# Mixer and MLP block: the first two tiles centred before the first product and scaled behind it, w1 loaded in quarters, two tiles transposed by DMA

## Chip, cores and metric

The kernel runs on one core of a Trainium2 chip. The metric is the device time of one launch in microseconds (us); smaller is better. Before the change three runs took 138.89, 138.96 and 139.11, median 138.96.

## What is computed

For x of 2048 rows by 512 columns, bfloat16, with weights w1, w2 (512 x 512), w3 (512 x 1792) and w4 (1792 x 512):

```python
h = gelu(layernorm(x) @ w1)              # layernorm over a row, no scale or offset
# the four column quarters g0..g3 of h are shifted by -1, +1, -2, +2 rows, zeros at the ends
hs = concatenate([g0, g1, g2, g3], axis=-1) @ w2
x1 = x + hs
out = x1 + gelu(layernorm(x1) @ w3) @ w4
```

layernorm is (x - mean) / sqrt(var + 1e-5), gelu its tanh approximation.

## The kernel before, in words

**Tiles.** Row r of x is row r // 16 of tile r % 16, so there are 16 tiles of 128 rows, and a shift of the rows by one is a step to the neighbouring tile. A product needs its input with the 512 columns on the partitions, so each normalized tile (xn) is transposed into xT, in one of two ways: four TensorE transposes into a PSUM bank and a copy out by ScalarE (ACT), steps tp (line 456) and evA (468); or a DMA transpose that SyncE (SP) issues, dT (444).

**Layernorm of a tile.** VectorE (DVE) takes statistics (st, 328) and makes mean and variance of them (ag, 331). GpSimd (POOL) adds epsilon and takes the power -1/2 (rs, 354 and 363, for one tile or two). DVE subtracts the mean and multiplies by that (norm, 434). For tile 2 the sums are taken by ACT instead (sum, dev, with vp, vpd and pw on POOL).

**First product** (m1, 507). A pair of tiles is taken at once: w1's blocks are the stationary operand, xT of the pair (256 columns) the moving one, so h comes out transposed, in two PSUM banks, and one gelu on ACT (g1, 568) writes it to hT. Pair 0 (m1x, 524) is computed tile by tile and input block by input block, 128 columns at a time, into four banks; its gelu is three instructions (551, 557), since tiles 0 and 1 lie next to zero columns.

**Second product** (m2, 582). For an output tile t it adds four matmuls, one for each shifted quarter j, which read hT of tiles t-1, t+1, t-2 and t+2. DVE adds x to the result (add, 594), which is x1, and the tiles are normalized again, mostly on ACT (424), and transposed by DMA into x1T.

**Third and fourth product** (609 and 635). Groups of four tiles: w3 against x1T, gelu on ACT (622), then w4, and DVE's last addition (649). From 37 us on nothing else runs on TensorE.

**The order.** Every engine runs its own list in program order and waits by semaphores; what waits for what follows from buffers read and written. The order of the front is written out by hand in HEAD, a list of steps that each append to one engine's list: `tp 0 4` transposes tile 0 into bank 4, `m1x 1 0 2` multiplies tile 1 with input block 2 in the banks from 0, `m1 2 0 3` makes output block 3 of pair 2 in the banks from 0, `m2 5 7 0 1 2 3` is tile 5 in bank 7 with all four quarters. Behind HEAD the order is in calls (lines 762 to 799). All loads are issued by SP, before HEAD: x tiles 0, 1, 2 and 3 one at a time, 4 and 5 together, w1 in two halves, x in 6-7, 8-9, 10-11, 12-15, then w2; w3 follows behind the last transpose of x. w4 comes in four pieces, among the transposes of the last tiles of x1.

**Warm-ups.** keep_warm (667) puts matmuls of ones into a bank nobody reads: 12 at the start, and 2 more (`warm 2 3 1`) between the transposes of tiles 0 and 1.

The start of HEAD, which sets who is behind whom:

```python
st 0; ag 0; rs 0 1; st 1; ag 1; sum 2; st 3; rs 1 1; norm 0; ag 3; tp 0 4; dev 2; vp 3; vpd 2;
st 4; evA 0; norm 1; warm 2 3 1; pw 2 2; tp 1 5; st 5; m1x 0 0 0; m1x 0 0 1; norm 2; evA 1;
```

Of the kernel before, what the change touches and what calls it, by code (L numbers as in the profile page):

```python
# [5 lines left out]
P = 128  # L6
# [4 lines left out]
LN_EPS = 1e-5  # L11
# [149 lines left out]
st 0; ag 0; rs 0 1; st 1; ag 1; sum 2; st 3; rs 1 1; norm 0; ag 3; tp 0 4; dev 2; vp 3; vpd 2;  # L161
st 4; evA 0; norm 1; warm 2 3 1; pw 2 2; tp 1 5; st 5; m1x 0 0 0; m1x 0 0 1; norm 2; evA 1;
m1x 0 0 2; norm 3; ag 4; tp 2 6; ag 5; m1x 0 0 3; rs 4; tp 3 7; evA 2; m1x 1 0 0; st 6;
m1x 1 0 1; m1x 1 0 2; evA 3; m1x 1 0 3; st 7; ag 6; ag 7; m1 1 4 0; rs 6; norm 5; g1 0; norm 4;
m1 1 4 1; tp 5 7; tp 4 6; st 8; evA 5; norm 7; m1 1 4 2; m1 1 4 3; evA 4; st 9; tp 7 7; ag 8;
ag 9; rs 8; norm 6; m1 2 0 0; evA 7; m1 2 0 1; st 11; tp 6 6; g1 1; m1 2 0 3; norm 8; ag 11;
m1 2 0 2; evA 6; m2 2 4 0; st 10; m2 2 4 1; norm 9; ag 10; m1 3 2 1; g1 2; rs 10; m1 3 2 3;
st 13; m1 3 2 0; st 12; ag 13; m1 3 2 2; norm 11; m2 2 4 2; dT 8; m2 2 4 3; st 14; g1 3; norm 10;
m2 3 5 0 1 2 3; dT 9; st 15; ag 12; ag 15; ag 14; rs 12; m2 4 6 0 1 2 3; m1 4 0 1; add 2; dT 11;
m1 4 0 0; rs 14; norm 13; m1 4 0 3; m1 4 0 2; add 3; norm 15; dT 10; norm 14; m2 5 7 0 1 2 3;  # L170
g1 4; norm 12; dT 13; dT 12; dT 15; dT 14
# [3 lines left out]
def bass_standalone__mixer_s_mlp__prompt_kernel(  # L175
# [18 lines left out]
    NO = 4  # L194

# [6 lines left out]
    with ExitStack() as es:  # L202
# [5 lines left out]
        hT = sb("hT", [P, DC, HTW], BF16)  # L208
        h2T = sb("h2T", [P, FC, 2, 512], BF16)
# [5 lines left out]
        sink = sb("sink", [P, D], BF16)  # L215
        tot = sb("tot", [P, NT, 2], F32)
# [117 lines left out]
        g_sd, g_sum, g_nm, g_dev = {}, {}, {}, {}  # L334
        g_vp = [None] * NT
        sink_slot = Slot()
# [35 lines left out]
        def sum_act(q):  # L372

            a, g = src(q)
            g_sum[q], g_nm[q] = Gen(), Gen()
            gs = sink_slot.new()
            pr.op("act", f"sq_sum{q}",
                  lambda e: e.activation(sink[:], a, ACT_F.Identity, accum_out=tot[:, q, 0:1]),
                  r=[g], w=[gs, g_sum[q]])
            pr.op("pool", f"nm{q}",  # L380
                  lambda e: e.tensor_scalar(nmean[:, q : q + 1], tot[:, q, 0:1], -1.0 / D, None,
                                            ALU.mult),
                  r=[g_sum[q]], w=[g_nm[q]])

        def dev_act(q):

            a, g = src(q)
            gs, gd = sink_slot.new(), Gen()
            pr.op("act", f"sq_dev{q}",
                  lambda e: e.activation(sink[:], a, ACT_F.Square, bias=nmean[:, q : q + 1],  # L390
                                         scale=1.0, accum_out=tot[:, q, 1:2]),
                  r=[g, g_nm[q]], w=[gs, gd])
            g_dev[q] = gd

        def vpe_dev(q):

            g_vp[q] = Gen()
            pr.op("pool", f"vpe{q}",
                  lambda e: e.tensor_scalar(vpe[:, q : q + 1], tot[:, q, 1:2], 1.0 / D, LN_EPS,
                                            ALU.mult, ALU.add),  # L400
                  r=[g_dev[q]], w=[g_vp[q]])

        def vpe_bn(q):

            g_vp[q] = Gen()
            pr.op("pool", f"vpe{q}",
                  lambda e: e.tensor_scalar(vpe[:, q : q + 1], mv[:, q : q + 1, 1], LN_EPS, None,
                                            ALU.add),
                  r=[g_mv[q]], w=[g_vp[q]])

        def pow2(q, n):

            pr.op("pool", f"pow{q}",
                  lambda e: e.tensor_tensor(rstd[:, q : q + n], vpe[:, q : q + n],
                                            neghalf[:, 0:n], ALU.pow),
                  r=g_vp[q : q + n] + [g_nh], w=g_rstd[q : q + n])

        def norm(eng, q):
            a, g = src(q)
            s = q % NXN  # L420
            g_xn[q] = xn_slot[s].new()
            if eng == "act":
                pr.op("act", f"norm{q}",
                      lambda e: e.activation(xn[:, s, :], a, ACT_F.Identity,  # L424
                                             bias=nmr[:, q : q + 1], scale=rstd[:, q : q + 1]),
                      r=[g, g_nmr[q], g_rstd[q]], w=[g_xn[q]])
            elif q in g_nm:
                pr.op(eng, f"norm{q}",
                      lambda e: e.tensor_scalar(xn[:, s, :], a, nmean[:, q : q + 1],
                                                rstd[:, q : q + 1], ALU.add, ALU.mult),  # L430
                      r=[g, g_nm[q], g_rstd[q]], w=[g_xn[q]])
            else:
                pr.op(eng, f"norm{q}",
                      lambda e: e.tensor_scalar(xn[:, s, :], a, mv[:, q, 0:1], rstd[:, q : q + 1],  # L434
                                                ALU.subtract, ALU.mult),
                      r=[g, g_mv[q], g_rstd[q]], w=[g_xn[q]])
# [78 lines left out]
        def mm1_tile_by_input(t, b, dc):  # L515

            p = t // 2
            if p not in g_y:
                g_y[p] = ([bank[b + i].new() for i in range(DC)], b)

            def f(e):
                for fc in range(DC):
                    o = 512 * (b + fc) + P * (t % 2)
                    ins = e.matmul(ps[:, o : o + P], w1_sb[:, dc, P * fc : P * (fc + 1)],  # L524
                                   xT[:, dc, P * t : P * (t + 1)],
                                   start=(dc == 0), stop=(dc == DC - 1))
                return ins

            pr.op("pe", f"m1x_{t}_{dc}", f, r=[g_w[("w1", dc)], g_xT[t]], w=g_y[p][0])
# [42 lines left out]
        g_o = {}  # L572

        def mm2(t, b, js=(0, 1, 2, 3)):

            if t not in g_o:
                g_o[t] = (bank[b].new(), b)
            win = [window(j, t) for j in js]

            def f(e):  # L580
                for j, (c, _) in zip(js, win):
                    ins = e.matmul(bankap(b), hT[:, j, c : c + P], w2_sb[:, j, :],  # L582
                                   start=(j == 0), stop=(j == DC - 1))
# [91 lines left out]
        load_x("sp", 2, 1)  # L675
        load_x("sp", 3, 1)
        load_x("sp", 4, 2)
        load_w("w1", w1_sb, w1, 0, 2)
        load_w("w1", w1_sb, w1, 2, 2)
        load_x("sp", 6, 2)  # L680
        load_x("sp", 8, 2)
        load_x("sp", 10, 2)
# [4 lines left out]
        keep_warm(12, 3)  # L687
# [55 lines left out]
        def last_tile():  # L743
# [10 lines left out]
            "warm": lambda n, b, q: keep_warm(n, b, [g_mv[q]]), "sum": sum_act, "dev": dev_act,  # L754
            "vpd": vpe_dev, "vp": vpe_bn, "pw": pow2, "m1x": mm1_tile_by_input,
            "m1": lambda p, b, *fcs: mm1(p, b, fcs), "g1": gelu1,
# [10 lines left out]
        mm2s(4, 4)  # L767
# [13 lines left out]
        for k in (10, 12, 14):  # L781
# [3 lines left out]
            load_w4(2 * (k - 10), 4)  # L785
        wide(0, [2, 3])
        load_w4(12, FC - 12)
# [44 lines left out]
```

## Time and profile before

| | us |
|---|---|
| median of three runs | 138.96 |
| the profiled execution | 138.48 |
| its span, first to last instruction | 136.6 |
| TensorE (PE) busy | 132.6 (97%) |
| VectorE / ScalarE / GpSimd busy | 50.9 / 51.7 / 18.8 |
| TensorE in the chain that ended last | 93% of the span |
| TensorE's first transpose of tile 0 / of tile 1 | 5.88 / 7.87 |
| first matmul of the third product | 37.33 |

The span is shorter than the execution's time by what lies around it (1.88). A line of the timeline gives start and length in us, engine, line of the kernel, operation, out<-in, form and count; in brackets stands how long the engine had been idle before it and who ended that. PEld is TensorE's loading of the stationary operand, which runs beside PE. The length of a PE instruction is from its issue to the end of its result, so lengths overlap; the pitch from one to the next is what counts for a sum. A table by stretch gives for each engine the busy time and the number of instructions, then the granted clock, the share of the DMA engines and GB/s. The DMA view gives for the issues of one kind the KB and the time from issue to landing.

### The profile page before, as it was taken

The numbers are of one execution on the slowest core, as the hardware profiler recorded it, in microseconds if no ns is written. First come the engines' busy times: TensorE is split into PE (matmuls) and PEld (weight loads), VectorE is DVE, ScalarE is ACT, GpSimd is POOL, SyncE is SP. The second block draws the span as 40 slices with busy tenths as digits, with TensorE's granted clock in tenths as the row PEclk, the third lists the DMA queues.
The fourth block names the chain that finished last, engine by engine and source line by source line (L and its number), as shares of the span: only waits on it lengthen the run. The fifth ranks groups of instructions, "written<-read, shape, count | busy, mean of one in ns | idle before, by whom it ended". The sixth has DMA issues, their size and how long they took to land.

```text
span 136.6 us, 1835 instructions
## 1 busy us (share of the span) xinstructions
PE 132.6 (97%) x716; PEld 67.3 (49%) x716; DVE 50.9 (37%) x125; ACT 51.7 (38%) x64; POOL 18.8 (14%) x52
## 2 busy tenths in 40 slices
PE   7979999999999999999999999999999999999993
PEld 3369857664444444444444444444444444444452
DVE  2699889999966610000322000023200002322222
ACT  4558623499535555552000555200055530000000
POOL 2644431553322200000000000000000000000000
PEclk9999999999999999999999999999999999999999
DMA  4996153499845499300111100011110001111121
GB/s 106 275 307 238 38 101 74 96 286 294 174 96 113 89 268 243 135 5 0 38 38 38 38 5 0 0 38 38 38 38 0 5 0 38 38 38 38 39 78 42
DMA packets 20264, 12.18 MB, mean 89 GB/s; under 512 B 13728, under 2 KB 19104, under 8 KB 20256
## 3 DMA queue, kind: packets, MB, share of 16 engines
q1 hardware_dynamic: 20112, 12.03, 33.3%
q8 instruction: 6, 0.10, 0.3%
q10 hardware_dynamic: 144, 0.03, 0.1%
q14 instruction: 2, 0.02, 0.1%
HBM read 6.82 MB, written 2.10 MB: 65 GB/s over the span
## 4 chain that ended last, share of the span: by engine, by line
PE 93%; DMA 3%; SPq 1%; DVE 1%; issue 0%
PE ps L635 35%; PE ps L609 35%; PE ps L582 10%; PE ps L507 9%; DMA x_sb<-in_x_dram 3%; PE ps L524 1%; PE ps L456 1%; SPq L258 1%; DVE st L328 1%; DVE xn L434 0%; DVE o_sb L649 0%
## 5 line engine op out<-in xcount | busy, mean ns | idle before, releaser
L635 PE MATMUL ps<-w_sb,h2T 128*128 128x512 bf16 (+2 forms) x238 | 48.9, 366 | 0.0
L609 PE MATMUL ps<-x1T,w_sb 128*128 128x512 bf16 x224 | 48.8, 379 | 0.0
L622 ACT ACTIVATE h2T<-ps 128x1024 bf16<-128x1024 f32 x28 | 28.7, 1024 | 44.8 <-PE ps L609 44.8
L649 DVE TENSOR_TENSOR o_sb<-ps,x_sb 128x512 bf16<-128x512 f32 (+2 forms) x17 | 11.2, 660 | 75.0 <-PE ps L635 75.0
L635 PEld LDWEIGHTS ps<-w_sb,h2T 128*128 128x128 bf16 x238 | 22.7, 98 | 26.0
L609 PEld LDWEIGHTS ps<-x1T,w_sb 128*128 128x128 bf16 x224 | 22.0, 98 | 26.4
L328 DVE BATCH_NORM_STATS2 st<-x_sb 128x6 f32<-128x512 bf16 x31 | 20.2, 680 | 2.9 <-DMA x_sb<-in_x_dram 2.9
L582 PE MATMUL ps<-w_sb,hT 128*128 128x512 bf16 x64 | 14.8, 379 | 0.0
L507 PE MATMUL ps<-xT,w_sb 128*128 128x256 bf16 x112 | 13.7, 273 | 0.0
L507 PEld LDWEIGHTS ps<-xT,w_sb 128*128 128x128 bf16 x112 | 10.7, 98 | 2.3 <-ACT xT L468 0.2
L363 POOL TENSOR_TENSOR rstd<-vpe,neghalf 128x2 f32<-128x2 f32 (+1 forms) x16 | 11.2, 699 | 0.9
L594 DVE TENSOR_TENSOR x_sb<-ps,x_sb 128x512 bf16<-128x512 f32 x16 | 10.3, 678 | 0.3 <-PE ps L582 0.2
L434 DVE TENSOR_SCALAR xn<-x_sb,mv,rstd 128x512 bf16<-128x512 bf16 x21 | 8.0, 404 | 4.5 <-POOL rstd L363 4.4
L582 PEld LDWEIGHTS ps<-w_sb,hT 128*128 128x128 bf16 x64 | 6.2, 98 | 6.3 <-ACT hT L568 0.3
L424 ACT ACTIVATE xn<-x_sb,nmr,rstd 128x512 bf16<-128x512 bf16 x10 | 7.5, 808 | 3.3 <-POOL nmr L368 3.3
L568 ACT ACTIVATE hT<-ps 128x1024 bf16<-128x1024 f32 x6 | 6.1, 1020 | 5.6 <-PE ps L507 5.6
L354 POOL TENSOR_SCALAR vpe<-mv 128x2 f32<-128x2 f32 (+1 forms) x16 | 3.7, 230 | 25.9 <-DVE mv L331 25.7
L667 PE MATMUL ps<-const-bfloat16-1.0 128*128 128x512 bf16 x14 | 6.0, 602 | 0.8 <-PEq L817 0.8
L468 ACT ACTIVATE xT<-ps 128x512 bf16<-128x512 bf16 x8 | 4.6, 597 | 2.2 <-PE ps L456 2.2
L331 DVE BATCH_NORM_AGGREGATE mv<-st 128x2 f32<-128x6 f32 x31 | 4.7, 172 | 0.1
L456 PE MATMUL ps<-ident,xn 128*128 128x128 bf16 x32 | 3.2, 231 | 0.9 <-DVE xn L434 0.9
L667 PEld LDWEIGHTS ps<-const-bfloat16-1.0 128*128 128x128 bf16 x14 | 1.9, 144 | 3.5 <-issue 3.5
(27 smaller groups left out, 17.2 us busy)
## 6 DMA issues: line engine op xcount, KB each, us to landing
w_sb<-in_w_dram SPq DMA_DIRECT2D x4, 512.0 KB, 4.4
out_dram<-o_sb SPq DMA_DIRECT2D x15, 128.0 KB, 1.8
w_sb<-in_w_dram SPq DMA_DIRECT2D x1, 1792.0 KB, 8.5
x_sb<-in_x_dram SPq DMA_DIRECT2D x4, 256.0 KB, 5.5
w_sb<-in_w_dram SPq DMA_DIRECT2D x3, 256.0 KB, 4.5
x_sb<-in_x_dram SPq DMA_DIRECT2D x4, 128.0 KB, 2.5
x_sb<-in_x_dram SPq DMA_DIRECT2D x1, 512.0 KB, 7.0
x1T<-xn SPq DMA_TRANSPOSE x16, 2.9
```

The lines of the kernel that those rows point to most:

```text
L328: pr.op("dve", f"st{q}", lambda e: e.bn_stats(st6[:, q, :], a), r=[g], w=[g_st[q]])
L363: lambda e: e.tensor_tensor(rstd[:, q : q + n], vpe[:, q : q + n], neghalf[:, 0:n], ALU.pow),
L424: lambda e: e.activation(xn[:, s, :], a, ACT_F.Identity, bias=nmr[:, q : q + 1], scale=rstd[:, q : q + 1]),
L434: lambda e: e.tensor_scalar(xn[:, s, :], a, mv[:, q, 0:1], rstd[:, q : q + 1], ALU.subtract, ALU.mult),
L507: ins = e.matmul(dst, w1_sb[:, dc, P * fc : P * (fc + 1)], xT[:, dc, 256 * p : 256 * (p + 1)], start=(dc == 0), stop=(dc == DC - 1))
L582: ins = e.matmul(bankap(b), hT[:, j, c : c + P], w2_sb[:, j, :], start=(j == 0), stop=(j == DC - 1))
L594: lambda e: e.tensor_tensor(x1_sb[:, t, :], bankap(b), x_sb[:, t, :], ALU.add),
L609: ins = e.matmul(bankap(b + i), w3_sb[:, dc, P * fc : P * (fc + 1)], x1T[:, dc, 512 * s : 512 * (s + 1)], start=(dc == 0), stop=(dc == DC ...
L622: pr.op("act", f"g2_{s}_{fp}", lambda e: e.activation(o, a, ACT_F.Gelu_apprx_tanh), r=gens, w=[g])
L635: ins = e.matmul(ps[:, 512 * b : 512 * b + n], h2T[:, fc, s % 2, P * i : P * (i + 1)], w4_sb[:, fc, c0 : c0 + n], start=(fc == 0), stop=(f ...
L649: lambda e: e.tensor_tensor(o_sb[:, s, 0:n], ps[:, 512 * b : 512 * b + n], x1_sb[:, t, c0 : c0 + n], ALU.add),
L667: ins = e.matmul(bankap(b), ones[:, 0:P], ones, start=True, stop=True)
```

## The change

For tiles 0 and 1 DVE only subtracts the mean (cen). The centred tile is transposed and multiplied with w1 the other way round: xT's block is the stationary operand, w1's rows (512 columns) the moving one (m1c, four matmuls for each tile), so y comes out with its rows on the partitions, and the gelu (gc) scales by each row's rstd as it reads. Four transposes (tph) and two copies (ehA) bring h of such a tile to hT. Pair 1 is now made tile by tile (m1t). The sums of tile 2 by ACT are gone, with the second warm-up; the first has 10 matmuls. w1 comes in four quarters among the x tiles 3, 4 and 5, x 8 to 11 in one load, w4 in two pieces. Tiles 6 and 7 are transposed by DMA. The second product's quarters are issued one by one, in any order within a tile. The rest of HEAD is written anew around this.

```diff
 HEAD = """
-st 0; ag 0; rs 0 1; st 1; ag 1; sum 2; st 3; rs 1 1; norm 0; ag 3; tp 0 4; dev 2; vp 3; vpd 2;
-st 4; evA 0; norm 1; warm 2 3 1; pw 2 2; tp 1 5; st 5; m1x 0 0 0; m1x 0 0 1; norm 2; evA 1;
-m1x 0 0 2; norm 3; ag 4; tp 2 6; ag 5; m1x 0 0 3; rs 4; tp 3 7; evA 2; m1x 1 0 0; st 6;
-m1x 1 0 1; m1x 1 0 2; evA 3; m1x 1 0 3; st 7; ag 6; ag 7; m1 1 4 0; rs 6; norm 5; g1 0; norm 4;
-m1 1 4 1; tp 5 7; tp 4 6; st 8; evA 5; norm 7; m1 1 4 2; m1 1 4 3; evA 4; st 9; tp 7 7; ag 8;
-ag 9; rs 8; norm 6; m1 2 0 0; evA 7; m1 2 0 1; st 11; tp 6 6; g1 1; m1 2 0 3; norm 8; ag 11;
-m1 2 0 2; evA 6; m2 2 4 0; st 10; m2 2 4 1; norm 9; ag 10; m1 3 2 1; g1 2; rs 10; m1 3 2 3;
-st 13; m1 3 2 0; st 12; ag 13; m1 3 2 2; norm 11; m2 2 4 2; dT 8; m2 2 4 3; st 14; g1 3; norm 10;
-m2 3 5 0 1 2 3; dT 9; st 15; ag 12; ag 15; ag 14; rs 12; m2 4 6 0 1 2 3; m1 4 0 1; add 2; dT 11;
-m1 4 0 0; rs 14; norm 13; m1 4 0 3; m1 4 0 2; add 3; norm 15; dT 10; norm 14; m2 5 7 0 1 2 3;
-g1 4; norm 12; dT 13; dT 12; dT 15; dT 14
+st 0; st 1; ag 0; ag 1; rs 0; st 2; cen 0; ag 2; rs 2 1; tp 0 4; st 3; ag 3; evA 0; cen 1;
+rs 3 1; tp 1 5; st 4; m1c 0 0 0; ag 4; m1c 0 0 1; evA 1; m1c 0 0 2; norm 2; rs 4 1; m1c 0 0 3;
+norm 3; m1c 1 1 0; tp 2 6; gc 0; tp 3 7; st 5; m1c 1 1 1; norm 4; evA 2; ag 5; rs 5 1; m1t 2 4 2;
+evA 3; st 7; tp 4 6; m1c 1 1 2; m1t 3 4 1; st 6; ag 7; m1c 1 1 3; ag 6; m1t 3 4 0; rs 6; norm 5;
+m1t 3 4 3; gc 1; m1t 2 4 0; m1t 2 4 3; st 8; tp 5 7; evA 4; m1t 3 4 2; m1t 2 4 1; st 9; evA 5;
+tph 1 3; norm 7; tph 0 2; ag 8; ag 9; m1 2 0 2; rs 8; g1 1; st 13; m1 2 0 3; ehA 0; norm 6;
+m1 2 0 0; ehA 1; st 11; m1 2 0 1; norm 8; m2 2 4 0; ag 11; m2 4 6 2; m2 3 5 0; st 10; m2 3 5 2;
+dT 7; g1 2; ag 10; m2 4 6 0; m2 5 7 2; rs 10; norm 9; ag 13; m2 3 5 1; m2 3 5 3; m2 2 4 1; st 12;
+m2 2 4 2; dT 6; m2 2 4 3; m2 4 6 1; norm 10; norm 11; ag 12; m1 3 2 1; rs 12; m1 3 2 3; st 14;
+dT 8; m1 3 2 2; add 2; m1 3 2 0; m2 5 7 0; m2 6 4 2; add 3; m2 6 4 0; dT 9; norm 12; m2 7 5 2;
+g1 3; m1 4 0 3; st 15; m2 7 5 0; norm 13; m2 4 6 3; ag 15; ag 14; dT 11; m2 5 7 1; rs 14;
+m1 4 0 0; m1 4 0 1; m2 5 7 3; m2 6 4 1; dT 10; norm 15; m1 4 0 2; norm 14; dT 13; g1 4; dT 12;
+dT 15; dT 14
 """
...
+        def mm1_tile(t, b, fc):
...
+                    ins = e.matmul(ps[:, o : o + P], w1_sb[:, dc, P * fc : P * (fc + 1)],
+                                   xT[:, dc, P * t : P * (t + 1)],
+                                   start=(dc == 0), stop=(dc == DC - 1))
...
+        def centre(q):
...
+            pr.op("dve", f"cen{q}",
+                  lambda e: e.tensor_scalar(xn[:, s, :], a, mv[:, q, 0:1], None, ALU.subtract),
+                  r=[g, g_mv[q]], w=[g_xn[q]])
...
+        def mm1_centred(t, b, dc):
...
+            pr.op("pe", f"m1c_{t}_{dc}",
+                  lambda e: e.matmul(bankap(b), xT[:, dc, P * t : P * (t + 1)], w1_sb[:, dc, :],
+                                     start=(dc == 0), stop=(dc == DC - 1)),
+                  r=[g_w[("w1", dc)], g_xT[t]], w=[g_yc[t][0]])
...
+        def gelu_scaled(t):
...
+                  lambda e: e.activation(hN[:, t, :], bankap(b), ACT_F.Gelu_apprx_tanh,
+                                         bias=0.0, scale=rstd[:, t : t + 1]),
+                  r=[g, g_rstd[t]], w=[g_hn[t]])
...
+        def peTh(t, b):
...
+                    ins = e.transpose(ps_bf[:, o : o + P], hN[:, t, P * c : P * (c + 1)], ident[:])
...
+        def evacH(eng, t):
...
+            for k, js in enumerate({0: ((0, 2), (1, 3)), 1: ((0, 1, 2), (3,))}.get(t, (range(DC),))):
...
+                pr.op(eng, f"eh{t}_{k}", f, r=[g], w=[g_h[(j, t // 2)] for j in js])
...
-                for j, (c, _) in zip(js, win):
+                for n, (j, (c, _)) in enumerate(zip(js, win), n0):
                     ins = e.matmul(bankap(b), hT[:, j, c : c + P], w2_sb[:, j, :],
-                                   start=(j == 0), stop=(j == DC - 1))
+                                   start=(n == 0), stop=(n == DC - 1))
...
         load_x("sp", 2, 1)
+        load_w("w1", w1_sb, w1, 0, 1)
         load_x("sp", 3, 1)
-        load_x("sp", 4, 2)
-        load_w("w1", w1_sb, w1, 0, 2)
-        load_w("w1", w1_sb, w1, 2, 2)
+        load_w("w1", w1_sb, w1, 1, 1)
+        load_x("sp", 4, 1)
+        load_w("w1", w1_sb, w1, 2, 1)
+        load_w("w1", w1_sb, w1, 3, 1)
+        load_x("sp", 5, 1)
         load_x("sp", 6, 2)
-        load_x("sp", 8, 2)
-        load_x("sp", 10, 2)
+        load_x("sp", 8, 4)
         load_x("sp", 12, 4)
         load_w("w2", w2_sb, w2)
...
-        keep_warm(12, 3)
+        keep_warm(10, 3)
...
         ln2a(0), ln2b(0)
-        mm2s(4, 4)
+        mm2(6, 4, (3,))
+        mm2(7, 5, (1, 3,))
...
-            load_w4(2 * (k - 10), 4)
+            if k < 14:
+                load_w4(7 * (k - 10) // 2, 7)
         wide(0, [2, 3])
-        load_w4(12, FC - 12)
```

## Prediction

> **What bounds the kernel now.** I read the chain of waits first, in order of time (start, length, what).
>
> ```profile
> 2.58 4.20 DMA x_sb<-in_x_dram
> ...
> 6.80 0.69 DVE st L328
> 7.50 0.33 DVE xn L434
> ...
> 7.87 0.40 PE ps L456 x4
> 8.27 0.67 PE ps L524 x12
> ...
> 37.50 24.17 PE ps L609 x112
> ```
>
> The load of tiles 4 and 5 lands at 6.78, DVE takes its statistics, and only then normalizes tile 1, which stands behind them in DVE's order. At 7.87 TensorE starts on that tile and never stops again. The table by stretch, for PE alone, says so:
>
> ```profile
> 7.87:28.68 20.81, 20.81 (x188) 1.00 0.53 136
> ```
>
> The work of that stretch by pitch: 0.2158 us for a 512-wide matmul (24.17/112), 0.109 for 256 (1.75/16), 0.0556 for 128 (0.89/16). Seven tiles of transposes 1.56, 32 matmuls of tiles 0 and 1 1.78, five pairs of the first product 8.72, and the pair before them 1.74, 32 matmuls of the second product 6.91: 20.7. Idle is 0.1. So there are two ways to gain, less PE work or an earlier 7.87, and a third wall behind: the third product needs w3 and four transposes behind it. The issues by DMA (KB, us to landing; w3 is issued at 26.21, the fourth transpose at 31.71):
>
> ```profile
> w_sb<-in_w_dram SPq DMA_DIRECT2D x1, 1792.0 KB, 8.5
> ```
> ```profile
> x1T<-xn SPq DMA_TRANSPOSE x1, 5.1
> ```
>
> They land at 34.7 and 36.8. The first matmul of the third product starts at 37.33, so a faster front alone can bring 0.5 at most.
>
> **Work.** Same to 0.1. Tiles 6 and 7 leave TensorE (8 transposes), h of tiles 0 and 1 enters (8). 32 matmuls of 128 (1.78) become 8 of 512 (1.73); pair 1 goes from 16 of 256 (1.74) to 32 of 128 (1.78). Second-product matmuls are only reordered. Sum 0.
>
> **The start.** x0, x1, x2 keep their places: issue plus time to landing gives 2.9, 3.6, 4.15. DVE by its pitches (0.61 from one statistics to the next instruction, 0.73 to its own aggregate, 0.31 for a normalization): st 0 2.95, st 1 3.60, ag 0 4.21, ag 1 4.32, st 2 4.41, cen 0 5.02 to 5.42. Centring waits for no POOL. I price it like the two-operation row, 0.40, between the aggregate's 0.17 and that. Its cover: norm 0 ended at 5.83 before. x3 is now fifth in the queue. Before, ten units of 128 KB had landed by 8.25 and four by 4.80, 0.575 each; so x3 5.4, x4 6.5, w1's quarters 4.8, 6.0, 7.1, 7.7, x5 8.25, and x6 on as before. (Bounds for a quarter: 2.7 us after its issue, as the single x tile, and 4.7, as the w1 half: the last at 7.2 to 9.2; I take the byte count.) st 3 5.42, ag 3 6.15, cen 1 6.24 to 6.64 (POOL's rs 2, 3 and 4, now one by one, end at 6.5, 7.5 and 8.5, ahead of norm 2 at 7.4, 3 at 7.7, 4 at 8.9), TensorE's dense work from **6.69: -1.18**.
>
> **The gaps that follow.** Hand-overs by rows: transposes to ACT 0.43 (7.87 to 8.30), ACT to PE 0.06, a product's last slot to ACT 0.2. ACT's own pitch is 0.49 for 512 columns, 0.31 for 256, 0.90 for 1024, from the timeline (start, length):
>
> ```profile
> 10.56 0.60 ACT L557 ACTIVATE hT<-ps 128x512 bf16<-128x512 f32 x1 [0.25 <-PE ps L524]
> 11.05 0.66 ACT L551 ACTIVATE hT<-ps 128x256 bf16<-128x256 f32 x2
> 11.67 1.08 ACT L468 ACTIVATE xT<-ps 128x512 bf16<-128x512 bf16 x2
> ```
>
> 1. Last w1 quarter 7.7 against PE at 7.56: 0.1.
> 2. gc 0 stands ahead of evA 2 on ACT. From the end of m1c 0's last slot: 0.2, gc 0 0.49, evA 2 0.60, 0.06 make 1.35; PE has m1c 1 0, two tiles of transposes and m1c 1 1 for it, 0.88: **0.47** (PE waits 8.8 to 9.27). gc 0 I price at 0.60 as L557; with a scale read per partition L424 took 0.81 from SBUF, which would add 0.2.
> 3. evA 5, g1 1, ehA 0 (two of 256), ehA 1 (384, then 128) in a row: from tp 5 at T = 11.25: 0.43 + 0.49 + 0.90 + 0.62 + 0.49 + 0.06 = T + 2.99. PE has T + 2.85: 0.14. Behind ehA 1 stands g1 2, done at 15.4; m2 3 5 1 comes to it at 15.5. The copies of 384 I put at 0.49, between 0.38 (256) and 0.60.
> 4. m2 6 4 2 needs bank 4, that is add 2 on DVE. x8 to x11 land at 11.1, as the sixteenth unit did. From there DVE is dense: st 8 11.2, norm 7 12.4 to 12.8, norm 6 to 14.0, norm 8 14.5, norm 9 15.7, norm 10 17.0 (POOL's pow), st 14 17.75, add 2 18.36 to 19.05, add 3 to 19.66. PE is there at T + 7.54 = 18.79. Waits **0.3**, and 0.18 more for add 3.
>
> Gaps 1.2, less the 0.1 of now.
>
> **SP's queue.** It takes dT 7 at 12.85 and dT 6 ahead of the eight there were; a transpose is issued every 1.31 and lands 2.5 later. xT 6 is there at 16.7, used at 16.8; 9 at 19.3, used 19.9; 10 at 21.9, used 22.8; 12 at 24.8, used 25.2. dT 13 waits for norm 13 (20.9), w3 goes out at 26.2, as now. No gap, but margins of 0.1 to 0.9 us, and w3 with its transposes holds the third product to 36.8. w4 in two pieces comes out on the same queue early, over 15 us ahead of 61.67: nothing.
>
> **Sum.** -1.18 + 1.2 - 0.1 = -0.1 on the profiled execution (138.48: span 136.60 and 1.88 around it), 138.4 there. The three runs' median, 138.96, lies 0.48 above the profiled one, so **138.85**. 0.2% (0.28 us) is about what a measurement of this kernel tells from no change. This forecast's own range is -0.4 to +0.3.
>
> **Rivals.**
>
> *DVE is earlier than I walk it.* x5 or x8 to x11 land 0.4 earlier (4 KB runs instead of 2 KB), adds 2 and 3 no longer wait, -0.5. Then w3's wall decides: about 138.4. Against: DVE carries st 2 that ACT had (+0.6).
>
> *TensorE's clock (the slower side).* PE's weight loads show two speeds:
>
> ```profile
> 4.98 0.15 PEld L667 LDWEIGHTS ps<-const-bfloat16-1.0 128*128 128x128 bf16 x1 [0.28 <-issue]
> 5.88 0.35 PEld L456 LDWEIGHTS ps<-ident,xn 128*128 128x128 bf16 x4 [0.75 <-DVE xn L434]
> ...
> 7.87 0.23 PEld L456 LDWEIGHTS ps<-ident,xn 128*128 128x128 bf16 x4 [1.43 <-DVE xn L434]
> ```
>
> The warm-ups run at a pitch of 0.427, twice 0.2158, up to 5.4, and four transposes that took 0.35 at 5.88 take 0.23 at 7.87. So full speed came between 5.9 and 7.9, after some 5 us of nearly unbroken work, while nothing needed it. The clock column shows 1.00 from 0 on and is blind to this; at the other end of the run it shows a fall:
>
> ```profile
> 134.24:136.20 1.96, 0.00 (x0) 0.00 (x0) 0.29 (x1) 0.00 (x0) 0.00 (x0) 1.00 0.23 67
> 136.20:136.60 0.40, 0.00 (x0) 0.00 (x0) 0.00 (x0) 0.00 (x0) 0.00 (x0) 0.51 0.00 0
> ```
>
> Idle for 1.96 us, then half speed. The change takes 4 of 14 warm-ups: ten end at 0.76 + 4.27 = 5.03, then PE is idle to 5.47, works 0.4 on tile 0, is idle to 6.69. Before the rise PE had done about 5.5 us of slow work (0.76 to 6.2). If the ten warm-ups and tile 0 (4.7) still count, it rises 0.8 after 6.69, at 7.5, which costs nothing once add 2 sets the pace; if the gaps undo them, 5.5 after, at 12.2, which walked through puts tp 5 at 13.4 and the sum at +1.6. I take the middle, 9.9: tp 1 6.69 to 7.12, m1c 0 to 8.83, m1c 1 0 to 9.26, tp 2 and 3 to 10.0, evA 2 to 10.51, m1t 10.57, tp 5 at 12.56 instead of 11.25. Add 2 no longer makes PE wait, which returns 0.48: net +0.8 to +0.9, **139.75**. It decides from a rise later than 7.5. For it: the cover goes where it was thinnest. Against: the executions shown, 138.48 to 139.11, are close together, and the gaps are each under 0.8.
>
> [...]
>
> *SP is held.* The transpose at 31.71 occupied SP for 2.88 instead of 1.27, with w3 and three transposes before it in flight. If dT 7, issued while w2 (to 13.8) is, is held so, w3 goes out 1.6 later, its wall is 38.4, and the sum +1.1: 140.0. Against: there is a third of w3's bytes ahead, and one transpose.
>
> That the change does not start earlier at all (tile 1 later than 7.87) needs x3 to land at 6.6, over 4 us after its issue; only the double tile took that.
>
> **How the numbers follow.** Forecast 0.46 (within 0.32, faster 0.10, slower 0.04), DVE early 0.17 (faster 0.16), clock 0.29 (slower 0.27), SP 0.08 (slower 0.07). Faster 0.26, within 0.2% 0.36, slower 0.38. The range runs from DVE early, 138.35, to SP and the clock's 9.9 with a quarter us on it, 140.0; outside lie the clock's late end and the ends of the others, about 0.18.
>
> **What would show it.** The first L456 transposes near 5.5 and the second near 6.7; their weight loads 0.23 for four if the clock is up, 0.4 if not, and m1c at 0.216 or 0.427; a PE gap of 0.4 to 0.5 ahead of the first m1t, released by ACT; one ahead of m2 6 4 2, released by DVE; w3 issued at 26.2 and the first L609 at 37.2. Wrong would be a dense PE from 6.7 on, PE waiting for w1 by more than 0.5, or an L609 that waits for a DMA.

## The result, and the profile after

The changed kernel took 140.82 us (median of 4 runs, 140.34 to 140.98), the one before 138.93 beside it (138.89 to 139.11): ratio 1.0125 [1.0097, 1.0153]. The forecast, 138.85, said no change, and its range ended at 140.0; the change is slower by 1.25%. Here and below a ratio is to the kernel before, run beside on the same chip, and runs over 1.5% above the fastest of their kernel are left out of it, so it can stand below that of the medians. The profiled execution of the changed kernel took 140.98, its span is 139.1 where it was 136.6: 2.5 longer.

The chain of waits of the changed kernel, in order of time (start, length, what), no longer runs through TensorE's front:

```profile
5.92 7.04 DMA x_sb<-in_x_dram
...
13.59 0.68 DVE st L330
...
17.89 0.68 POOL rstd L363
18.57 3.65 DMA xT<-xn
...
22.35 0.60 PE ps L456 x4
...
39.90 24.33 PE ps L621 x112
```

Read from the bottom: the third product starts at 39.90 (37.33 before, so +2.57, the whole loss). TensorE had waited at 22.35 for a transpose of tile 9 that took 3.65 from its issue at 18.57. The step of POOL ahead of it only ends at the same time: tile 9 had been normalized by 17.73, and its transpose waited for SP, which was issuing tile 8's.

```profile
17.35 0.38 DVE L383 TENSOR_SCALAR xn<-x_sb,mv,rstd 128x512 bf16<-128x512 bf16 x1
```
```profile
17.26 1.26 SPq L393 DMA_TRANSPOSE xT<-xn  x1
```

SP issued without a break from the first transpose on, and that one was held up by DVE, which had waited for x tiles 8 to 11, a load of 7.04 that landed at 12.96. The table by stretch, for PE alone, from tile 1's transposes to the third product (stretch, its length, PE's busy time, count, granted clock, DMA share, GB/s):

```profile
6.78:39.90 33.12, 30.72 (x228) 1.00 0.77 178
```

Tile 1 starts 1.09 earlier than before, but the stretch is 33.12 long instead of 29.46. So 3.66 of waits has been put in. The timeline of PE names them (in brackets the idle time and who ended it):

```profile
6.78 0.40 PE L405 MATMUL ps<-ident,xn 128*128 128x128 bf16 x4 [0.82 <-DVE xn L489]
...
8.12 0.60 PE L498 MATMUL ps<-w_sb,xT 128*128 128x512 bf16 x2 [0.30 <-DMA w_sb<-in_w_dram]
...
9.78 0.40 PE L473 MATMUL ps<-xT,w_sb 128*128 128x128 bf16 x4 [0.39 <-ACT xT L417]
...
15.64 2.75 PE L594 MATMUL ps<-w_sb,hT 128*128 128x512 bf16 x12 [0.83 <-DMA w_sb<-in_w_dram]
...
20.75 0.99 PE L594 MATMUL ps<-w_sb,hT 128*128 128x512 bf16 x3 [0.16 <-DVE x_sb L606]
...
22.35 0.60 PE L456 MATMUL ps<-xT,w_sb 128*128 128x256 bf16 x4 [0.61 <-DMA xT<-xn]
```

A bracket counts from the end of the last result, which is about 0.16 behind the moment at which the next matmul could have been issued (0.38 long, 0.2158 apart). With that, w1's last quarter costs 0.46, ACT 0.55, **w2 1.0**, the adds 0.5, **tile 9's transpose 0.75**, and 0.23 is lost at tile 6's; together 3.5 of the 3.66. The start, w1, ACT and the adds were in the forecast's sum in some size. w2 and the transpose were not. DVE's timeline shows where the row of transposes is made late:

```profile
12.98 1.29 DVE L330 BATCH_NORM_STATS2 st<-x_sb 128x6 f32<-128x512 bf16 x2 [1.79 <-DMA x_sb<-in_x_dram]
```

Tile 7's normalization stands behind these statistics in DVE's order, so its transpose, the first on SP, is issued at 14.61 and not at 12.85. The DMA view of the two late loads (KB, us from issue to landing), of x tiles 8 to 11 and then of w2, in the windows of their issue:

```profile
x_sb<-in_x_dram SPq DMA_DIRECT2D x1, 512.0 KB, 7.0
```
```profile
w_sb<-in_w_dram SPq DMA_DIRECT2D x1, 512.0 KB, 8.7
```

Issued at 5.92 and 6.87, they land at 12.9 and 15.57 (a landing is the issue plus the view's time, which is given to 0.1). Before, x 8-9 landed at 10.55, 10-11 at 11.13 and w2 at 13.80. The first ten units of 128 KB had landed by 8.37 (8.23 before) and twelve by 9.04 in both, give or take 0.05, so up to there nothing was later. The table by stretch shows how much was moved behind that (the last two columns are the DMA engines' share and GB/s), for the kernel before:

```profile
5.00:9.00 4.00, 3.12 (x29) 1.00 1.02 296
9.00:12.00 3.00, 3.00 (x47) 1.00 0.97 362
```

and the changed one:

```profile
5.00:9.00 4.00, 2.32 (x21) 1.00 0.85 257
9.00:12.00 3.00, 2.61 (x39) 1.00 0.91 316
12.00:15.60 3.60, 2.81 (x36) 1.00 0.32 118
```

39 GB/s less over 4 us and 46 less over 3 make 0.29 MB that had still to come at 12.0. The DMA engines weren't full while the quarters and single tiles were fetched (0.85 for 1.02), and the rest trickled in at 118 GB/s.

Last, the slow transposes. The DMA view between 18.3 and 19.9, where those of tiles 8 and 9 are in flight:

```profile
q8 instruction: 1, 0.02, 5.9%
issues: line engine op xcount, KB each, median us to landing
xT<-xn SPq DMA_TRANSPOSE x2, 3.9
```

and SP's timeline there:

```profile
18.57 2.35 SPq L393 DMA_TRANSPOSE xT<-xn  x1
```

One packet of 16 KB on the queue called instruction, 1.5 us long, falls among them at 18.34. They land 4.2 and 3.6 after their issue where 2.5 is usual, and the second holds SP for 2.35 instead of 1.27: 1.08, by which everything behind it on SP is later, w3 last (28.83 instead of 26.21). In the kernel before such a packet came at 13.4, ahead of the first transpose (14.86), with nothing to disturb.

### The profile page after: what moved, and what is told of

The parts are those of the page before. It is cut to its first block, busy times and chain, and to the rows that moved or that the text cites. A ratio compares the mean times of both kernels' runs of the same rounds, so it can differ in the third digit from the quotient of the medians.

```text
span 139.1 us, 1816 instructions
## 1 busy us (share of the span) xinstructions
PE 132.2 (95%) x704; PEld 65.5 (47%) x704; DVE 51.3 (37%) x127; ACT 50.2 (36%) x61; POOL 18.9 (14%) x52
## 4 chain that ended last, share of the span: by engine, by line
PE 82%; DMA 8%; SPq 3%; DVE 3%; issue 1%; POOL 1%
PE ps L621 35%; PE ps L647 35%; PE ps L594 7%; PE ps L456 5%; DMA x_sb<-in_x_dram 5%; DMA xT<-xn 3%; SPq L260 2%; DVE st L330 2%; SPq L267 1%; DVE xn L383 1%; POOL rstd L363 0%; DVE mv L333 0%; POOL vpe L354 0%; DVE o_sb L661 0%
## 5 line engine op out<-in xcount | busy, mean ns | idle before, releaser
L330 DVE BATCH_NORM_STATS2 st<-x_sb 128x6 f32<-128x512 bf16 x32 | 20.8, 678 | 4.2 <-DMA x_sb<-in_x_dram 4.2
L594 PE MATMUL ps<-w_sb,hT 128*128 128x512 bf16 x64 | 15.3, 379 | 1.0 <-DMA w_sb<-in_w_dram 0.8
L363 POOL TENSOR_TENSOR rstd<-vpe,neghalf 128x2 f32<-128x2 f32 (+1 forms) x18 | 12.3, 686 | 1.1
L456 PE MATMUL ps<-xT,w_sb 128*128 128x256 bf16 x96 | 11.6, 273 | 0.7 <-DMA xT<-xn 0.6
L456 PEld LDWEIGHTS ps<-xT,w_sb 128*128 128x128 bf16 x96 | 9.2, 98 | 3.3 <-DMA xT<-xn 1.6
L383 DVE TENSOR_SCALAR xn<-x_sb,mv,rstd 128x512 bf16<-128x512 bf16 x20 | 7.5, 403 | 5.1 <-POOL rstd L363 5.1
L417 ACT ACTIVATE xT<-ps 128x512 bf16<-128x512 bf16 x6 | 3.4, 595 | 4.4 <-PE ps L405 4.4
L679 PE MATMUL ps<-const-bfloat16-1.0 128*128 128x512 bf16 x10 | 4.2, 597 | 0.8 <-PEq L831 0.8
L405 PE MATMUL ps<-ident,xn 128*128 128x128 bf16 x24 | 2.2, 220 | 1.4 <-DVE xn L489 1.4
L498 PE MATMUL ps<-w_sb,xT 128*128 128x512 bf16 x8 | 2.6, 380 | 0.3 <-DMA w_sb<-in_w_dram 0.3
(25 smaller groups left out, 18.3 us busy)
```

The source lines that it names most:

```text
L330: pr.op("dve", f"st{q}", lambda e: e.bn_stats(st6[:, q, :], a), r=[g], w=[g_st[q]])
L456: ins = e.matmul(dst, w1_sb[:, dc, P * fc : P * (fc + 1)], xT[:, dc, 256 * p : 256 * (p + 1)], start=(dc == 0), stop=(dc == DC - 1))
```

## Experiments

**Theories.** *A, loads:* the new cut of the loads brings x 8-11 and w2 late. *B, instruction block:* the 16 KB packet is a piece of TensorE's instruction stream; the change moved it into the row of transposes. *C, two more transposes* on SP are the loss by themselves. *D, clock:* fewer warm-ups, later full speed. *E, the new order* (centred tiles, products by tile) costs by itself. The first number under each experiment is the median in us, the second the ratio with its 95% interval, and times are those of the profiled execution.

**x 8-11 in two loads (A).**

```diff
-        load_x("sp", 8, 4)
+        load_x("sp", 8, 2)
+        load_x("sp", 10, 2)
```

> The changed kernel (140.8), with the load of x tiles 8 to 11 cut in two again (8-9, 10-11). Loads theory: in the changed kernel DVE stood idle 1.79 us for that load (landed 12.96; tiles 8 and 9 were there by 10.5 before), and norm 7, norm 6 and SP's transposes came late by as much. Cut in two, tiles 8 and 9 land near 11.8, the first DMA transpose is issued at 13.5 instead of 14.6, the third product starts 0.8 to 1.2 earlier: 139.6 to 140.0. Transposes theory (ten DMA transposes in a row on SP where there were eight, 2 x 1.31 = 2.6 us, set the end): the row starts earlier, so a gain too, but not over 0.5, since tile 8 and 9's long landing stays: 140.3 to 140.8.

139.85, 1.0072 [1.0041, 1.0103]. x 8-9 landed at 10.81, w2 at 15.03, the third product started at 38.41. Some of the loss is probably that one load, though the interval just touches that of the change. The block, the 16 KB packet, fell at 17.79 and the transposes beside it still took 4.2 and 3.4, one holding SP for 2.31. In the profiled execution the clock fell to half from 7.40 to 10.82, so the size is blurred.

**Tiles 6 and 7 back to TensorE and ACT (C).**

```diff
-dT 7; g1 2; ... st 12; m2 2 4 2; dT 6; m2 2 4 3; ...
+g1 2; ... tp 7 0; evA 7; st 12; m2 2 4 2; tp 6 1; evA 6; m2 2 4 3; ...
```

> The changed kernel (140.8), with tiles 6 and 7 transposed by TensorE and copied by ACT again (banks 0 and 1, behind the first second-product matmuls), all else as changed. Transposes theory: eight transposes on SP instead of ten, tile 8's issued at 15.7 instead of 17.3 and w3 at 26.5 instead of 28.8; the waits of PE for tile 6 (0.2) and tile 9 (0.75) go, 0.44 of PE work comes: 139.8 to 140.2. Loads theory: the waits for w2 (1.0), for the last w1 quarter (0.46) and for add 2 and 3 (0.5) stay, so no better than that, and 140.3 if the adds come no earlier.

140.67, 1.0123 [1.0068, 1.0177]: nothing gained that shows. The block, at 16.47, fell on the issue of the first transpose, which took 2.7 (SP 1.60); the one that took longest, 3.6, had a packet of 8 KB beside it. x 8-11 landed at 12.90, w2 at 15.55. TensorE takes on 0.44 of work here, which hides a gain of that size. C alone does not carry the loss.

**The kernel before with the new loads (A against E).** In before's code only the load calls of the change.

> The kernel before (138.9), with the changed kernel's loads alone: w1 in quarters among tiles 3, 4 and 5, which come one by one, and 8 to 11 in one load. Loads theory: DVE waits for tile 8 here too (lands near 12.9 against 10.5), and w2 lands near 15.5 where the first second-product matmul was due at 14.8: slower by 1 to 2 us, 140.0 to 141.0, in spite of tile 4 landing earlier. If the loss is in the order of the work: within 0.4 of 138.9, since TensorE's start is then 0.3 to 0.8 earlier.

139.63, 1.0079 [1.0051, 1.0107]. x 8-11 at 13.01, w2 at 15.55, third product at 39.20. In the kernel before, the loads alone bring two thirds of the loss, without any of the new order.

**The instruction block moved (B).** 40 warm-ups of 128 columns for 10 of 512: the same time, 30 matmuls more, so that the block comes earlier if it goes by how many TensorE has started.

```diff
-                    ins = e.matmul(bankap(b), ones[:, 0:P], ones, start=True, stop=True)
+                    ins = e.matmul(ps[:, 512 * b : 512 * b + P], ones[:, 0:P], ones[:, 0:P],
+                                   start=True, stop=True)
...
-        keep_warm(10, 3)
+        keep_warm(40, 3)
```

> The changed kernel (140.8), with the 10 warm-ups of 512 columns made 40 of 128 columns: the same time on TensorE, but 60 more instructions ahead of the rest. In the changed kernel a 16 KB block on the queue for instructions took 1.5 us at 18.34 while the transposes of tiles 8 and 9 were in flight; these took 4.2 and 3.6 us to land instead of 2.5, and PE waited 0.75 for tile 9. Fetch theory: the block is TensorE's next instructions, and it moves to near 14; both transposes land in 2.5, SP is not held at tile 9 (1.27 instead of 2.35): 0.5 to 1.0 faster, 139.8 to 140.3. If the block is not it: the landing stays at 4.2 and 3.6, and the time at 140.8 within 0.2.

139.66, 1.0066 [1.0036, 1.0097]. The DMA view of 12.4 to 13.9, then of 18 to 20:

```profile
q8 instruction: 1, 0.02, 3.8%
```
```profile
xT<-xn SPq DMA_TRANSPOSE x3, 2.5
```

The block is at 12.51, the transposes of x take 2.5 (one 2.8), SP's issues 1.3 or less, w3 goes out at 27.64 (28.83), the third product at 38.88 (39.90). Nothing else was touched, so that the block held them is shown; its price, about 0.8 us (0.0059 of 138.7), is less sure, since the two ratios' intervals meet at 1.0097. PE still waits 1.04 for w2, which lands at 15.46: A is untouched by it.

**The changed kernel with the loads of before (A).**

```diff
-        load_w("w1", w1_sb, w1, 0, 1)
         load_x("sp", 3, 1)
-        load_w("w1", w1_sb, w1, 1, 1)
-        load_x("sp", 4, 1)
-        load_w("w1", w1_sb, w1, 2, 1)
-        load_w("w1", w1_sb, w1, 3, 1)
-        load_x("sp", 5, 1)
+        load_x("sp", 4, 2)
+        load_w("w1", w1_sb, w1, 0, 2)
+        load_w("w1", w1_sb, w1, 2, 2)
         load_x("sp", 6, 2)
-        load_x("sp", 8, 4)
+        load_x("sp", 8, 2)
+        load_x("sp", 10, 2)
```

> The changed kernel (140.8) with the loads ahead of w2 put back as they were before: x 4-5 together, w1 in two halves, 8-9 and 10-11. Loads theory: w2 is issued at 6.2 instead of 6.87 and lands near 13.8 instead of 15.57, tiles 8 and 9 near 10.6 instead of 12.9; the first matmul of the first product waits for w1's first half (7.46), 0.5 later than with quarters. PE's wait for w2 (1.0) goes, the third product starts 1.2 to 1.8 earlier than at 39.9: 139.0 to 139.6. If the order of the work is the loss: 140.5 or more, since the start is later.

140.4, 1.0107 [1.0063, 1.015], with the runs apart: two took 139.19 and 139.21, the others 140.3 to 141.65. x 8-9 landed at 10.06, w2 at 13.39, tile 7's transpose was issued at 12.83, the forecast's 12.85. But tile 0's products now stand ahead of w1's halves, and the table by stretch shows what that did to the clock (third number from the right):

```profile
5.38:8.79 3.41, 1.33 (x10) 1.00 0.90 283
8.79:12.20 3.41, 3.37 (x20) 0.50 0.99 372
12.20:15.62 3.42, 3.42 (x52) 1.00 0.34 82
```

After a stretch with 1.33 us of recorded work the clock went to half for 3.41. The block, at 19.36, held transposes as well (4.8 and 4.0; SP 2.32). A is right on the landings; the time was eaten by two others.

**4 warm-ups for 10 (D).** `keep_warm(4, 3)`.

> The changed kernel (140.8) with 4 warm-ups instead of 10, nothing else. Clock theory: TensorE's clock rises at the earliest after the first product has begun (four transposes' weight loads take 0.4 instead of 0.23 at tile 0 and tile 1), by 10 us; if the clock set the pace in this kernel, 0.5 to 1.0 slower, 141.3 to 141.8. Loads theory: PE stands still for w2 to 15.6 in any case (1.0), so the slow clock ahead of it is hidden: 140.8 within 0.4.

139.97, 1.0097 [1.0071, 1.0123]: not slower, though the clock rose at 8.72 (4.54 in the changed kernel's profile). What TensorE loses in the front it would else have waited for w2, which here landed at 14.76, before TensorE came to it (15.08); D is not what makes the change slow.

**Split, block and ACT's order at once.** x 8-11 in two, 40 narrow warm-ups, and `evA 2; evA 3` ahead of `gc 0`.

> The changed kernel with three edits: 8 to 11 in two loads, the 40 narrow warm-ups (TensorE's instruction block earlier), and evA 2 and 3 ahead of gc 0 in ACT's order. Loads and fetch theories together: the gains of the two alone (about 1.0 and 1.2 on 140.8) add in part, since both act on the row of transposes and on the adds; w2 still lands near 15.0, as its issue stays at 7.3, and PE waits for it about 0.7 to 1.0: 138.9 to 139.5. The swap (PE idle 0.55 ahead of the first m1t) gives nothing while PE waits for w2. If the two are one loss seen twice: 139.7, no better than either.

139.86, 1.0097 [1.0062, 1.0132]. The block, now at 14.42, fell on w2's tail: w2 landed at 16.23, PE waited 1.73, and the first transpose took 3.6. ACT's gap shrank from 0.39 to 0.25. A block that is moved must be moved to where nothing is late.

**w1's quarters issued by ACT (A, the issue).** As above, and SP issues no w1.

> The kernel of the three edits, with w1's quarters issued from ACT's queue behind its table load instead of SP's. Issue theory: w2 lands 7.6 us after its issue before (6.20) and with 8 to 11 cut in two (7.33): it is late because 15 issues of 0.475 us stand on SP where there were 12. With 11 on SP, w2 is issued at 5.4 and lands at 13.3 to 13.8; PE does not wait for it; 138.0 to 138.7, faster than the kernel before or equal to it. Bandwidth theory (small pieces move slower, whoever issues them): w2 still lands near 15, no better than the three edits.

139.91, 1.011 [1.0069, 1.0151]. w2, issued at 5.43 instead of 6.87, landed at 13.13, 7.7 after its issue (7.6 in the kernel before): it is not late where the small pieces stand in another queue, and is where it stands behind them, as the last of 14 issues of 0.475. But x2 landed at 5.94, tile 0's transposes came at 6.95, the clock rose at 13.0, and the third product at 39.99. The early loads of x paid for it (the first w1 quarter was issued at 0.89, beside x0).

**The changed kernel again.**

> The changed kernel as it is, beside the next three on one chip, since single runs have spread by 1 to 2 us. 1.0125 of the kernel before, within its interval (1.010 to 1.015), with 8-11 landed at 12.9, w2 at 15.5 and the third product from 39.5 to 39.9, whatever TensorE's clock does.

140.66, 1.0121 [1.0082, 1.016]. In this execution x 8-11 landed at 11.91 and w2 at 14.46, a microsecond earlier than in the first, and the block, at 15.92, held two transposes for 4.1 and 3.6, for which PE waited 1.43. The same total by other parts: landings differ by 1 us between executions of one kernel.

**Other cuts of the loads.** w1 in halves and x 4-5 together behind x 3's place, x 8-11 in two, norm 2 and 3 ahead of st 4, narrow warm-ups; the second with `warm 6 3` behind tile 0's transposes; the third with x 4 and x 5 single.

> The changed kernel with its loads cut anew: x0, x1, x2, first half of w1, x3, second half of w1, x 4-5, 6-7, 8-9, 10-11, 12-15, w2 (12 issues on SP as before, w2 issued at 6.2), norm 2 and 3 ahead of st 4 on DVE, 40 narrow warm-ups (TensorE's instruction block near 12.5), evA 2 and 3 ahead of gc 0. Loads and fetch theories: 8-9 land near 10.6 and w2 near 13.6, no wait for either, all transposes land in 2.5, the third product starts at 36.9 to 37.5 where TensorE's clock is up by 7: 138.2 to 138.9, equal to the kernel before or faster. Clock theory: nothing hides the clock now, so runs split: those in which it rises late or falls again take 0.8 to 1.5 more (139.5 to 140), and the median lies between.

> The last kernel with six more narrow warm-ups between the transposes of tiles 0 and 1 (0.64 us at half speed, where TensorE stood idle for 0.7). Clock theory: from the ten profiles the clock rises when a stretch of 3.41 us had 77% or more of TensorE busy (74% was not enough) and falls at 34% or less (38% was enough to stay); six more lift the stretches that end at 6 to 7.5 from 60-70% to over 75%, so fewer runs are slow: median 0.2 to 0.6 under the last kernel's, at 138.2 to 138.7. If the split in runs is not the clock: no difference.

> The recut kernel with the cover, with tiles 4 and 5 loaded one by one: in the recut one the pair landed at 9.3 to 10.0, 5.7 to 6.4 us after its issue, norm 4 came 2.5 late, TensorE stood idle for tile 4, and its clock fell in nearly all runs. Alone, tile 4 lands near 7.2 and that wait goes. Loads and fetch theories: with 8-9 near 11 and w2 near 14.2, all transposes at 2.5, 138.4 to 139.3. If the order of the work loses by itself: 139.5 or more, with all loads in time.

141.88, 1.0189 [1.0147, 1.0232]; 141.77, 1.0106 [1.0042, 1.0169]; 139.59, 1.0045 [1.0014, 1.0076]. All three missed what was expected: in the first two, x 4-5 landed at 9.98 and 9.28, PE was idle for 2.47 and 2.13 ahead of tile 4, and in both the clock fell (13.07 to 16.49, 12.85 to 16.26). With single tiles PE still waited 1.65 there.

**The kernel before with 4 warm-ups.**

> The kernel before with 4 warm-ups instead of 12 and none between the transposes of tiles 0 and 1. Clock theory: TensorE works from 7.87 on without a gap there, so nothing hides a late rise: the clock rises at 10 to 12, and 2 to 4 us of work at half speed cost 1.0 to 2.0: 139.7 to 140.7. If warm-ups only fill idle time: 138.7 within 0.2.

140.04, 1.0066 [1.0041, 1.0091]. Slow clock up to 11.8, but also the block at 17.22 (transposes 4.0 and 3.5), where it was at 13.4 with all the warm-ups. Clock and block can't be told apart here.

**The kernel before with tile 1 normalized first.** `norm 1; evA 0; st 4` for `st 4; evA 0; norm 1`.

> The kernel before with one step moved on DVE: norm 1 ahead of st 4 (its rstd is there at 6.3, and it stood behind a load that lands at 6.78). TensorE's transposes of tile 1 at 6.8 instead of 7.87, its first product from w1's first half on (7.46 landed) instead of 8.05, the second half at 8.25. If TensorE's start sets the end there: 0.3 to 0.5 faster, 138.3 to 138.6, capped by w3's transposes (36.8) ahead of the third product. If what follows (w1's second half, tile 4's statistics) takes it back: 138.9 within 0.2.

138.88, 0.9997 [0.9973, 1.0021]. Tile 1 came at 6.87, 1.0 earlier, nearly all that the change was to win at the start, for one line. But PE then waited for w1's second half (8.74):

```profile
8.76 0.40 PE L524 MATMUL ps<-xT,w_sb 128*128 128x128 bf16 x4 [0.83 <-DMA w_sb<-in_w_dram]
```

The fourth transpose behind w3 landed at 37.66 and the third product started at 37.80 (37.33 before). The early start had no value here, with w1's second half landing behind it.

**Block moved and tiles 6, 7 by TensorE.**

> The kernel with the 40 narrow warm-ups (139.7), with tiles 6 and 7 transposed by TensorE as well. Loads theory: what is left over the kernel before (0.9) is the wait for w2 (1.0) and DVE's late start on tiles 8 to 11, and taking two transposes out of SP's row gives at most 0.3: 139.4 to 139.8. Transposes theory: the row of ten still sets the adds and the later pairs: 139.0 or less.

140.13, 1.0108 [1.007, 1.0146], no better than the block alone (1.0066). The next version, which keeps both transposes on SP and loses nothing that can be measured, takes C out.

**Old loads, block moved, clock covered, ACT's order.** The changed kernel with the loads of before, 40 narrow warm-ups, 6 more behind tile 0's transposes, 8 behind `m1c 0 0 1`, evA 2 and 3 ahead of gc 0.

> The changed kernel with the loads put back as before (w2 landed at 13.4 with them), 40 narrow warm-ups (TensorE's instruction block ahead of the transposes), six more behind tile 0's transposes and eight behind the second matmul of m1c 0, where PE waits for w1's second half (8.7), and evA 2 and 3 ahead of gc 0. Loads and fetch theories together, clock covered: the two together explain the whole loss, so 138.4 to 139.1, at the kernel before (139) or just under it. If the order of the work costs by itself: 139.5 or more, with w2, the transposes and the clock in time.

138.62 against 138.42, 1.0014 [0.9993, 1.0035]: no loss left that can be measured. Its stretch from tile 1 to the third product, and three lines of PE's timeline:

```profile
6.48:37.57 31.09, 29.81 (x232) 1.00 0.76 189
```
```profile
7.60 0.38 PE L498 MATMUL ps<-w_sb,xT 128*128 128x512 bf16 x1 [0.72 <-DMA w_sb<-in_w_dram]
...
10.00 0.40 PE L473 MATMUL ps<-xT,w_sb 128*128 128x128 bf16 x4 [0.25 <-ACT xT L417]
...
15.24 2.54 PE L594 MATMUL ps<-w_sb,hT 128*128 128x512 bf16 x11 [0.21 <-ACT hT L536]
```

The block is at 12.35, w2 lands at 13.92, w3 goes out at 25.67. The centred tiles are all still there, the new order too but for gc 0, now behind evA 3, and so are the two extra transposes: **C and E are out**, as far as the interval tells (0.35% at most is left). A and B, with the clock covered and gc 0 moved, make up the loss; the run does not part these four. Nor is there a gain: tile 1 is 1.39 earlier, and the first matmul of w1 waits 0.72 for the half that lands at 7.36; the kernel before, started as early, waited for w1 in the same way (0.83, above). No version that was run beats the kernel before.

## Why the prediction was wrong

**Right: the start.** Centring without POOL gave 6.78 (forecast 6.69), -1.09 for -1.18. x3, x4 and x5 landed at 5.59, 6.24 and 8.37 (5.4, 6.5, 8.25).

**Right: ACT's order.** gc 0 ahead of evA 2 cost 0.55 (0.47), and the adds 0.5 (0.48). In the second there is luck: DVE's add of tile 2 (20.02 for 18.36) and TensorE's coming to it (20.43 for 18.79) were both 1.6 later than forecast. The 0.14 behind ehA 1 is hidden in the changed kernel by the wait for w2; with w2 in time it is 0.21 of idle, 0.37 with the 0.16.

**Undersized: w1's last quarter.** It landed at 8.09, 3.6 after its issue, not 7.7; within the bounds of 7.2 to 9.2 that were stated. PE lost 0.46, not 0.1.

**Wrong: "x8 to x11 land at 11.1, as the sixteenth unit did".** This is the step that failed first. Sixteen units had landed by 11.13 in a queue of fewer loads, in which tiles 8 to 11 came as two. As one load behind the small ones they landed at 12.96, 1.9 late, and DVE stood still for 1.79. The 0.29 MB that the queue had moved less by 12.0 do not explain that by themselves. Cut in two behind the same small loads, 8-9 landed at 10.81 and 11.71 and 10-11 at 11.5 and 12.4 (the split alone, then with the block and ACT's order), and the split alone had moved as little by 12.0 (253 and 298 GB/s in the same two stretches). The one load landed at 11.9 to 13.0 in the seven profiles that have it, and tile 8's statistics, the first to use it, started at 12.98 in the changed kernel, when all four tiles were there (12.96). Why it lands later than two of half its size is not shown. Norm 7, and with it SP's whole row of transposes, moved by the same: 14.61 for 12.85 (+1.76).

**Wrong: w2 had no term.** The same byte count let it land as before (13.8). It went out 0.67 later and took 1.1 longer: 15.57, and PE waited 1.0 for it.

**Wrong: "a transpose is issued every 1.31 and lands 2.5 later".** Two transposes took 4.2 and 3.6, and SP lost 1.08. With the 1.76 of its late start this puts w3 at 28.83 (26.2 forecast) and the fourth transpose behind it at 39.73 (36.8): the forecast's third wall moved to within 0.2 of where PE arrives, so neither alone would have given the time back.

**The rivals.** *SP is held* named the right effect, a transpose that keeps SP for over a microsecond (1.6 forecast, 1.08 measured), but for a wrong reason: it put it on w2's and w3's bytes in flight. Tile 7's transpose, issued at 14.61 with w2 in flight to 15.57, kept SP for 1.30 and landed in 2.5. The transposes of x that took 3.1 and more, with no load beside them, had an instruction packet beside them, and moving the block freed them with the loads as they were. With bytes in flight alone SP was held as well, but by less: with w3 on its way and no block until SP was free again, a transpose kept SP for 2.04 (changed kernel, at 34.23; block at 37.12) and 2.07 (the last version, at 32.13). The 2.88 at 31.71 from which the rival was priced had both, w3 and a block at 31.19. *TensorE's clock* is real, since the rise and the fall did move with warm-ups and waits (a rise at 4.54 with 10 warm-ups and 8.72 with 4, a fall at 8.79 with the loads of before, where PE waited for w1's halves), but in the changed kernel's profile the rise was at 4.54 and tile 0's four weight loads took 0.23: it cost nothing there. *DVE earlier* did not happen: the 0.4 that it gave to runs of 4 KB was the author's estimate, which no run shows, and x 8 to 11, loaded in such runs, landed at 12.96 for the 11.1 of the forecast. Nor did *not starting earlier*. The sum, then: forecast -1.18 + 1.2 - 0.1, measured -1.09 + 3.66; of the 2.65 between them w2 has 1.0, tile 9's and tile 6's transposes 1.0, w1's quarter 0.36 and the start 0.09.

What stays open: how much the late loads cost by themselves in the changed kernel, since every version without them also changed the clock or the block; in the kernel before, that cost is 0.79% [0.51, 1.07]. So do what the cover of the clock and the move of gc 0 are worth in the last version, and why the landings of one kernel differ by a microsecond between executions.

## What to carry to other kernels

Walk each load by its issue time and by what is in flight, not by a count of bytes: here the smaller pieces landed their first bytes earlier (w1's first quarter at 4.81, the half at 7.46) and what stood behind them in the same queue later (w2 at 15.57 for 13.80), and the load of four tiles served the first of them at 12.96, where loads of two had it at 10.55 (before) and 10.81 (8-11 in two). Ask of an earlier start what it will wait for next; here the last of w1 landed about when it had before (8.09 for 8.23), and one moved line in the old kernel bought nearly the same start (6.87 for 6.78), and as little gain. And a change in the number of instructions moved the 16 KB packet here (30 matmuls more: 12.51 for 18.34), so look for such a packet in the DMA view beside any transfer that got slower without a cause of its own.

## What the runs showed of the hardware

**Instruction blocks held DMA transposes.** A 16 KB packet on the instruction queue, 0.9 to 1.6 us on one DMA engine, came when TensorE had started 96 to 112 recorded matmuls in fourteen of the eighteen profiles (77 to 128 in the other four), and the next after 211 to 243 in all. So it moved with the number of TensorE's instructions and with the waits ahead of it: 13.4 before, 18.34 and 15.92 in two executions of the changed kernel (w2 at 15.57 and 14.46), 12.51 with 30 matmuls more. A late w2 thus also put the block among the transposes. A transpose issued 1.0 to 1.9 us ahead of it took 3.6 to 4.8 instead of 2.5, and mostly so did the next one (3.4 to 4.1), with SP held up to 2.35 instead of 1.27. Where the block came within 0.1 of the row's first issue, that transpose landed in 2.5 (w1 by ACT, 13.76) and 2.7 (tiles 6 and 7 by TensorE, 16.47). A smaller packet (8 KB, 20 to 24) lies beside one transpose of 3.1 to 3.6 in ten of the eighteen, the kernel before included, and beside one of 2.8 or so in most others. That the large one is TensorE's stream is inferred from where it falls and from its move with 30 more matmuls; no record names its engine.

**The clock's stretches.** Thirteen of the profiles have a record of the clock's changes (the clock column shows 1.00 ahead of the first one). The time from one change to the next was a whole number of stretches of 3.413 us: 38 in the kernel before (rise at 6.50, fall at 136.21), 40 in the changed one (136.53 from the rise at 4.54), one at half speed with 8-11 in two (7.40 to 10.82), with the loads of before (8.79 to 12.20) and in the first two recuts (13.07 to 16.49, 12.85 to 16.26). The edges lay elsewhere in every execution: the rises at 4.54, 6.50, 8.72 (4 warm-ups) and 13.0 (w1 by ACT) are no whole number of stretches apart. The share of a stretch in which TensorE was busy, counting recorded matmuls by their pitch, sorts these changes. The clock rose behind shares of 0.75 (first recut), 0.77 (4 warm-ups) and 0.80 (second recut) and not behind 0.74 and 0.66 (tiles 6 and 7 by TensorE) and 0.68 (before). It fell behind 0.22 and 0.32 (the first two recuts), 0.24 (loads of before) and 0.34 (8-11 in two), and stayed behind 0.39 (changed), 0.41 (split, block and ACT's order) and 0.43 (before with the new loads). It fell, then, also behind stretches in which TensorE was up to a third busy: with the loads of before, 1.33 us of recorded work in 3.41 (0.24 by pitch) did not prevent it.
